# One small exponential per unit for the roots of queries and keys, and a least key root per unit for the flag

## Chip, cores, metric

One core of one Trainium2 chip. The metric is device time in microseconds (us). The kernel before takes 607.91 us (median of the 3 runs given at the start, 607.86 to 608.15).

Engines in the profile: PE is the matmul engine (TensorE), DVE VectorE, ACT ScalarE, POOL GpSimd. The granted clock is the share of its full clock that PE was given.

## The reference, cut to what matters

```python
def rmsnorm(x, g):                      # q, k: (8, 12, 448, 64)
    rms = np.sqrt(np.mean(x * x, axis=-1, keepdims=True) + 1e-06)
    return x / rms * g
q_n, k_n = rmsnorm(q, g_q), rmsnorm(k, g_k)
scores = 1/np.sqrt(64) * np.matmul(q_n, k_n.transpose(0, 1, 3, 2))
attn = softmax(scores)                  # cut
attn_out = np.matmul(attn, v)
# then, on (8, 448, 768): layer norm, ReLU MLP 768 -> 3072 -> 768, residual
```

Only the inverse root 1/rms of each query and key row is touched by the change. The kernel multiplies the queries by theirs, and passes the keys' as the per-row scale of the big exponential over the scores.

## The kernel before

The work on queries, keys and values goes in 25 units: the first two hold one pair of heads (7 groups of 128 rows for queries and 7 for keys), the others two pairs (14 and 14). A root is made as exp(-0.5 ln(sum of squares)) on ACT. A guard is computed at the end: if any root or sum lies outside what the fast path can represent, a flag sends the program to a slow general path. For that guard every key root of the whole kernel was kept in one tile `rr_all` of 336 columns.

```python
self.rr = fix.tile([128, 7 * B * NPAIR], FP32, name="rr_all", tag="rr_all")   # 336 columns
...
def begin():                                   # per unit u, g = 7 or 14 groups
    ...
    o = 7 * UNIT_PAIR[u]
    c["r", 0] = self.p_n.tile([128, 14], FP32, tag="rq", name="rq")[:, 0:g]   # queries
    c["r", 1] = self.rr[:, o:o + g]                                           # keys
...
def root(n=slice(0, 2)):
    nc.scalar.activation(c["rt"][:, n], c["ssq"][:, n], AFT.Ln, bias=D * 1e-6)
    for i in range(2)[n] if isinstance(n, slice) else (n,):
        nc.scalar.activation(c["r", i], c["rt"][:, i], AFT.Exp, scale=-0.5)
...
# scores(p, i): one 128 x 448 block of exp(scores), with the key root as scale
nc.scalar.activation(out=c["E"][:, i], in_=ps[:, 0:S], func=AFT.Exp,
                     scale=self.rr[:, g:g + 1], bias=EXP_BIAS)
...
# step "M" of the written order of instructions, at the end of the ramp
nc.vector.tensor_reduce(out=gmax, in_=self.sh.gprod, axis=AX.X, op=ALU.max, ...)
nc.vector.tensor_scalar(out=gmax, in0=gmax, scalar1=1.0 / K_MAX, ...)
...
# flag(), near the end: all key roots at least gmax?
nk = self.rr.shape[1]
nc.vector.tensor_scalar(out=good[:, 0:nk], in0=self.rr, scalar1=sh.gmax, scalar2=None, op0=ALU.is_ge)
nc.vector.tensor_reduce(out=cnt[:, 1:2], in_=good[:, 0:nk], axis=AX.X, op=ALU.add)
```

The order of instructions is written out by hand; only DVE after the first part is ordered by the scheduler. The order string at the end of the first part is `... l5 z5 U1 U2 V6.5 M m5 V6.6 L7 K7`, where `m5` is a copy of queries and `K7` the transpose and copy of keys whose result PE waits for.

## Time and profile before

| | kernel before |
|---|---|
| time | 607.91 us |
| span of the profiled run | 605.9 us |
| PE busy | 578.3 us (95%) |
| ACT busy | 360.7 us, 697 instructions |
| DVE busy | 286.5 us, 618 instructions |

The span is a ramp of about 61 us, in which PE waits for the others again and again, then 507 us in which it hardly waits, then the last block of matmuls and stores. The groups that the change removes or shrinks are small. From the view of groups by line and shape (count after the x; then busy us and mean ns; then the engine's idle time before them):

```profile
L223 ACT ACTIVATE rq<-rt 128x14 f32<-128x14 f32 x23 | 5.0, 215 | 0.7
L223 ACT ACTIVATE rr_all<-rt 128x14 f32<-128x14 f32 x23 | 4.5, 198 | 0.0
...
L741 DVE TENSOR_REDUCE cnt<-good 128x1 f32<-128x336 f32 x1 | 0.5, 493 | 0.0
...
L739 DVE TENSOR_SCALAR good<-rr_all,gmax 128x336 f32<-128x336 f32 x1 | 0.4, 395 | 0.1
```

The two groups of exponentials come to 9.5 us by these figures.

### The profile page before, as it was taken

The page shows a single profiled execution, that of the slowest core. Times are in us where ns is not written, and L with a number is a line of the kernel's source. Part 1 is how long each engine was busy: PE and PEld are TensorE (multiplying, and loading weights), DVE is VectorE, ACT ScalarE, POOL GpSimd, SP SyncE. Part 2 cuts the span into 40 slices and gives each one's busy share as a digit, 9 for nine tenths or more (in the row PEclk, how much of TensorE's full clock was granted, in tenths as well). Part 3 has the DMA queues.
Part 4 walks back from the last instruction along what each step waited for, and adds up shares of the span by engine and source line. Part 5 has one row for each costly group of instructions (what it writes and reads, how often), then busy time and mean ns, then how long its engine had stood idle before and what let it go on. Part 6 is the DMA issues. An engine that isn't in the chain of part 4 may idle for free.

```text
span 605.9 us, 11525 instructions
## 1 busy us (share of the span) xinstructions
PE 578.3 (95%) x4500; PEld 344.6 (57%) x4500; DVE 286.5 (47%) x618; ACT 360.7 (60%) x697; POOL 189.5 (31%) x245
## 2 busy tenths in 40 slices
PE   2877999999999999999999999999999999999995
PEld 1555666655566666655566666655566666654564
DVE  5799567734346256715256255734256322540011
ACT  6996986278752697358753598548754477124200
POOL 3853432233551355332542345423512000000000
PEclk9999999999999999999999999999999999999998
DMA  9999999479864586844944585847722330130011
GB/s 208 266 213 217 215 224 178 123 195 87 143 157 117 98 129 146 177 135 83 150 121 113 123 125 128 197 116 121 133 65 70 92 62 2 34 98 0 1 53 57
DMA packets 130861, 75.29 MB, mean 124 GB/s; under 512 B 96656, under 2 KB 121040, under 8 KB 130800
## 3 DMA queue, kind: packets, MB, share of 16 engines
q1 hardware_dynamic: 114048, 45.12, 38.3%
q0 software_dynamic: 16080, 28.94, 21.6%
q8 instruction: 37, 0.61, 0.4%
q10 hardware_dynamic: 672, 0.43, 0.2%
q14 instruction: 24, 0.20, 0.1%
HBM read 52.36 MB, written 11.01 MB: 105 GB/s over the span
## 4 chain that ended last, share of the span: by engine, by line
PE 88%; DVE 1%; ACT 1%; issue 0%
PE psC L637 36%; PE psH L621 34%; PE psS L352 8%; PE oA L381 5%; PE oB L383 2%; PE psS L356 1%; PE psS L355 1%; PE tr L330 0%; PE tr L316 0%; ACT E L358 0%; DVE x L398 0%; DVE qn L67 0%; DVE khl L240 0%; ACT khl L215 0%; ACT hT L623 0%
## 5 line engine op out<-in xcount | busy, mean ns | idle before, releaser
L621 PE MATMUL psH<-xnT,w 128*128 128x512 f16 (+1 forms) x1134 | 241.9, 353 | 0.0
L358 ACT ACTIVATE E<-psS,rr_all 128x448 f16<-128x448 f32 x336 | 207.0, 634 | 48.3 <-PE psS L352 43.0
L637 PE MATMUL psC<-w,hT 128*128 128x384 f16 (+1 forms) x1368 | 234.7, 323 | 0.0
L623 ACT ACTIVATE hT<-psH 128x512 f16<-128x512 f32 (+1 forms) x189 | 104.0, 550 | 123.9 <-PE psH L621 121.9
L637 PEld LDWEIGHTS <-hT 128*128 128x128 f16 x1368 | 127.5, 98 | 74.6
L621 PEld LDWEIGHTS <-w 128*128 128x128 f16 x1134 | 102.5, 98 | 80.9 <-issue 0.3
L352 PE MATMUL psS<-qU,kU 128*128 128x448 f16 x288 | 100.6, 357 | 8.3 <-ACT E L358 6.0
L381 PEld LDWEIGHTS <-E 128*128 128x128 f16 x1008 | 70.7, 98 | 49.1 <-issue 4.4
L229 POOL TENSOR_TENSOR qkv<-qkv,gprod 128x896 f32<-128x896 f32 x21 | 43.7, 2081 | 95.8 <-issue 49.5
L381 PE MATMUL oA<-v,E 128*128 128x65 f16 x864 | 66.7, 194 | 0.1
L641 DVE SCALAR_TENSOR_TENSOR x<-psC,rs_all,x 128x384 f32<-128x384 f32 x48 | 29.0, 616 | 71.5 <-PE psC L637 71.1
L396 DVE RECIPROCAL rec_all<-oA 128x6 f32<-128x6 f32 x48 | 9.3, 194 | 94.4 <-PE oA L381 94.2
L383 PE MATMUL oB<-v,E 128*128 128x65 f16 x288 | 51.9, 194 | 0.1
L127 POOL DMA_DIRECT2D qkv<-in_k_dram x14 | 11.2, 798 | 129.7 <-DVE qn L279 61.8
L218 DVE TENSOR_REDUCE ssq<-khl 128x14 f32<-128x896 f32 (+1 forms) x24 | 25.6, 1065 | 44.6 <-ACT khl L215 44.5
L352 PEld LDWEIGHTS <-kU 128*128 128x128 f16 x288 | 28.0, 98 | 25.5 <-issue 6.0
L218 DVE TENSOR_REDUCE ssq<-qn 128x14 f32<-128x896 f32 (+1 forms) x25 | 26.2, 1047 | 21.8 <-ACT qn L215 21.7
L67 DVE SCALAR_TENSOR_TENSOR qn<-qkv,rq 128x256 f16<-128x256 f32 (+1 forms) x72 | 26.3, 425 | 15.1 <-ACT rq L223 15.0
L383 PEld LDWEIGHTS <-E 128*128 128x128 f16 x336 | 32.5, 97 | 0.3 <-DVE xl L403 0.2
L240 DVE TENSOR_TENSOR khl<-qkv,khl 128x896 f16<-128x896 f32 x21 | 22.8, 1088 | 10.8 <-ACT khl L237 7.1
L398 DVE TENSOR_TENSOR x<-oA,rec_all 128x384 f32<-128x384 f32 x48 | 26.8, 558 | 1.5
L545 DVE BATCH_NORM_STATS2 stat<-x 128x6 f32<-128x256 f32 (+1 forms) x75 | 26.2, 404 | 0.6
(104 smaller groups left out, 447.7 us busy)
## 6 DMA issues: line engine op xcount, KB each, us to landing
out_dram<-x SPq DMA_DIRECT2D x20, 384.0 KB, 2.5
qkv<-in_k_dram POOLq DMA_DIRECT2D x14, 384.0 KB, 3.9
qkv<-in_q_dram POOLq DMA_DIRECT2D x14, 384.0 KB, 5.2
qkv<-in_v_dram POOLq DMA_DIRECT2D x14, 384.0 KB, 6.6
w<-in_moe_w_ch_dram POOLq DMA_DIRECT2D x3, 1536.0 KB, 14.6
w<-in_moe_w_ch_dram POOLq DMA_DIRECT2D x2, 2304.0 KB, 24.3
qkv<-in_k_dram SPq DMA_DIRECT2D x7, 384.0 KB, 5.7
qkv<-in_q_dram SPq DMA_DIRECT2D x7, 384.0 KB, 4.6
```

The costliest lines, as they stand in the source:

```text
L67: nc.vector.scalar_tensor_tensor(out=out, in0=x, scalar=8.0, in1=r.unsqueeze(2).broadcast_to([x.shape[0], g, D]), op0=ALU.mult, op1=ALU.mult)
L218: nc.vector.tensor_reduce(out=c["ssq"][:, n], in_=c["sq", n], axis=AX.X, op=ALU.add)
L229: (nc.vector if u in DVE_KG else nc.gpsimd).tensor_tensor(out=c["t"][1], in0=c["t"][1], in1=sh.gprod.unsqueeze(1).broadcast_to([128, g, D] ...
L352: nc.tensor.matmul(ps[:, 0:S], c["main"][:, ts(i, 128)], q[:, ts(h, S)], start=True, stop=True)
L358: nc.scalar.activation(out=c["E"][:, i], in_=ps[:, 0:S], func=AFT.Exp, scale=self.rr[:, g:g + 1], bias=EXP_BIAS)
L381: nc.tensor.matmul(oA[:, t, cs], E[:, i, ts(t, 128)], rhs, start=(i == 0 and t == 0), stop=(i == 6 and t == 2))
L383: nc.tensor.matmul(oB[:, cs], E[:, i, 320:448], rhs, start=(i == 0), stop=(i == 6))
L398: nc.vector.tensor_tensor(out=x[:, :, 128 * hp:128 * hp + 128].rearrange("p t (e d) -> p t e d", e=2), in0=oA[:, :, :, 0:D], in1=rec[:, 0: ...
L621: nc.tensor.matmul(ps[:, 0:N], sh.w1[:, dc, ts(f, 128)], xnT[:, dc, 0:N], start=(dc == 0), stop=(dc == NDC - 1))
L623: nc.scalar.activation(out=hT[:, f, 0:N], in_=ps[:, 0:N], func=AFT.Relu)
L637: nc.tensor.matmul(ps[:, 0:g[1]], hT[:, f, ts(t, 128)], sh.w2[:, f, cols], start=(f == 0), stop=(f == NFF - 1))
L641: nc.vector.scalar_tensor_tensor(out=x[:, cols], in0=ps[:, 0:g[1]], scalar=self.rs[:, b, t:t + 1], in1=x[:, cols], op0=ALU.mult, op1=ALU.add)
```

## The change

Its intent: one exponential for both roots in place of two, a small tile of roots per unit in place of columns of a big one, and only the least key root of each unit for the guard, so that the guard compares 25 columns and not 336. The price is one reduce per unit on DVE, five of them together at "M".

```diff
-        self.rr = fix.tile([128, 7 * B * NPAIR], FP32, name="rr_all", tag="rr_all")
+        self.rr = fix.tile([128, len(UNITS)], FP32, name="rr_all", tag="rr_all")
@@ begin
-            o = 7 * UNIT_PAIR[u]
-            c["r", 0] = self.p_n.tile([128, 14], FP32, tag="rq", name="rq")[:, 0:g]
-            c["r", 1] = self.rr[:, o:o + g]
+            c["rb"] = self.p_n.tile([128, 2, 14], FP32, tag="rq", name="rr_all", bufs=6)[:, :, 0:g]
+            c["r", 0], c["r", 1] = c["rb"][:, 0], c["rb"][:, 1]
@@ root
-            for i in range(2)[n] if isinstance(n, slice) else (n,):
-                nc.scalar.activation(c["r", i], c["rt"][:, i], AFT.Exp, scale=-0.5)
+            nc.scalar.activation(c["rb"][:, n], c["rt"][:, n], AFT.Exp, scale=-0.5)
@@ scores
-                             scale=self.rr[:, g:g + 1], bias=EXP_BIAS)
+                             scale=self.units[PAIR_UNIT[p][0]][3][:, g:g + 1], bias=EXP_BIAS)
+        u = PAIR_UNIT[p][0]
+        if i == 6 and UNIT_PAIR[u] == p and u > 4:
+            self.least(u)
+    def least(self, u):
+        self.nc.vector.tensor_reduce(out=self.rr[:, u:u + 1], in_=self.units[u][3], axis=AX.X,
+                                     op=ALU.min)
@@ step "M"
+                for u in range(5):
+                    self.least(u)
                 gmax = self.sh.gmax
```

More of the change, by code (lines that the diff above doesn't have):

```diff
@@ L201, in begin @@
             c["rt"] = self.p_n.tile([128, 2, 14], FP32, tag="rt", name="rt")[:, :, 0:g]
-            o = 7 * UNIT_PAIR[u]
-            c["r", 0] = self.p_n.tile([128, 14], FP32, tag="rq", name="rq")[:, 0:g]
-            c["r", 1] = self.rr[:, o:o + g]
+            c["rb"] = self.p_n.tile([128, 2, 14], FP32, tag="rq", name="rr_all", bufs=6)[:, :, 0:g]
+            c["r", 0], c["r", 1] = c["rb"][:, 0], c["rb"][:, 1]
             c["qn"] = self.p_n.tile([128, 14, 2, D], FP16, tag="qn", name="qn")[:, 0:g]
             c["khl"] = self.p_n.tile([128, 14, 2, D], FP16, tag="khl", name="khl")[:, 0:g]
-            self.units[u] = (c["qn"], c["khl"], m)
+            self.units[u] = (c["qn"], c["khl"], m, c["r", 1])
         def square(n):
@@ L310, in trans_k @@
         u, w = PAIR_UNIT[p]
-        qn, khl, m = self.units[u]
+        qn, khl = self.units[u][0:2]
         kT, ps = self.kU[PE_SET][:, 960 * (p % 2):960 * (p % 2) + 960], self.tr
@@ L322, in trans_q @@
         u, w = PAIR_UNIT[p]
-        qn, khl, m = self.units[u]
+        qn, khl = self.units[u][0:2]
         tr = self.ps_m.tile([128, 1024], FP16, tag="mlp", name="psQ") if p < NPAIR else self.tr
@@ L356, in scores @@
             nc.tensor.matmul(ps[:, 0:S], left[:, 64:192], q[:, S:2 * S], start=False, stop=True)
-        g = 7 * UNIT_PAIR[PAIR_UNIT[p][0]] + self.group(p, i)
+        g = self.group(p, i)
         nc.scalar.activation(out=c["E"][:, i], in_=ps[:, 0:S], func=AFT.Exp,
-                             scale=self.rr[:, g:g + 1], bias=EXP_BIAS)
+                             scale=self.units[PAIR_UNIT[p][0]][3][:, g:g + 1], bias=EXP_BIAS)
[5 more added lines that the diff above has]
+                                     op=ALU.min)
     def values(self, p, i):
```

## The prediction

> **What bounds the kernel now.** I read the page's busy table and slices first, then busy time by stretch, then TensorE's waits, then the instructions around the two places that the change touches. The page of the kernel before:
>
> ```profile
> PE 578.3 (95%) x4500; PEld 344.6 (57%) x4500; DVE 286.5 (47%) x618; ACT 360.7 (60%) x697; POOL 189.5 (31%) x245
> PE   2877999999999999999999999999999999999995
> ```
>
> TensorE (PE) is the bound on the whole; ScalarE (ACT) and VectorE (DVE) have slack on the average. But the first four digits are 2, 8, 7, 7: there are 605.9 - 578.3 = 27.6 us without PE work, and most of it lies in the first 60 us. The view by stretch shows the two regimes (columns: stretch, its length, busy us and instructions by engine, clock, DMA share, GB/s):
>
> ```profile
> 20.00:30.00 10.00, 7.84 (x100) 5.22 (x100) 8.59 (x17) 9.81 (x21) 8.10 (x10) 1.00 0.89 237
> 30.00:40.00 10.00, 8.41 (x110) 5.61 (x109) 9.65 (x20) 9.71 (x18) 5.95 (x7) 1.00 1.10 211
> 40.00:50.00 10.00, 7.00 (x95) 4.39 (x92) 9.46 (x27) 8.42 (x17) 5.11 (x3) 1.00 1.12 217
> ...
> 200.00:300.00 100.00, 100.00 (x769) 57.91 (x767) 45.86 (x103) 72.71 (x144) 44.77 (x62) 1.00 0.69 132
> ```
>
> In the ramp PE has 7 to 8.4 us of work in 10 while ACT and DVE are at 8.4 to 9.8: there a microsecond of ACT or DVE can be a microsecond of the kernel. From about 61 us on, attention and MLP matmuls are interleaved and PE is never short of work. After 60 us these are all of PE's listed waits:
>
> ```profile
> PE psS L352 <- DVE kU L318: 0.5, 1, 0.5
> PE psS L352 <- ACT E L358: 0.2, 1, 0.2
> ```
>
> So a change to small ACT and DVE instructions can act only in the ramp, up to that 0.5 us wait for a DVE copy at 60.9 us, which ends the ramp.
>
> [...] On ACT, for unit 2:
>
> ```profile
> 18.39 0.23 ACT L221 ACTIVATE rt<-ssq 128x28 f32<-128x28 f32 x1
> 18.65 0.22 ACT L223 ACTIVATE rq<-rt 128x14 f32<-128x14 f32 x1
> 18.77 0.20 ACT L223 ACTIVATE rr_all<-rt 128x14 f32<-128x14 f32 x1
> 18.88 2.21 ACT L358 ACTIVATE E<-psS,rr_all 128x448 f16<-128x448 f32 x4
> ```
>
> Each small exponential is recorded as 0.20 to 0.22 us, but the next instruction starts 0.11 to 0.12 us after it. The logarithm costs more (0.26), since the first exponential waits for its result. On DVE at the end of the ramp:
>
> ```profile
> 57.26 1.08 DVE L67 SCALAR_TENSOR_TENSOR qn<-qkv,rq 128x896 f16<-128x896 f32 x1
> 58.26 0.21 DVE L443 TENSOR_REDUCE gmax<-gprod 128x1 f32<-128x64 f32 x1
> 58.51 0.15 DVE L445 TENSOR_SCALAR gmax<-gmax 128x1 f32<-128x1 f32 x1
> 58.58 0.38 DVE L279 COPY qn<-qn 128x896 f16<-128x896 f16 x1
> ```
>
> The 896-column instruction holds the engine for 58.26 - 57.26 = 1.00 us. [...] the 0.15 us scaling of gmax is followed 0.07 us later. [...]
>
> **The change, part by part.** The ordered instruction lists of both kernels, with their semaphore waits, are alike on PE, GpSimd and the DMA queues; on ACT and DVE only the following differs.
>
> (a) ACT, removed: one exponential in 24 of the 25 units (the first unit's two roots are taken separately and stay two). The survivor has 28 columns in place of 14, some 0.02 us more (the logarithm's mean is 240 ns at 28 columns, 215 at 14). Not 24 x 0.2 = 4.8 us but about 24 x 0.10 = 2.4 us of engine time. Nineteen of these lie after 61 us, where PE does not wait: worth nothing. Unit 5's, at 56.75, lies in the ramp, but the DVE instruction that needs it starts at 57.26, long after. Units 1 to 4 fall at 13.3, 18.8, 28.8 and 40.9 us. From 23.9 to 44.4 us DVE has no idle time: it is the limit there, ACT's saving for unit 3 is lost behind it, and unit 4's runs into 0.54 us of ACT idle at 42.1. That leaves units 1 and 2, whose following score exponentials are what PE waits for (PE idle for ACT E at 14.9, 19.5 and 23.3 us). 2 x 0.10 = 0.2 us earlier at the most, 0.1 if another wait takes over: I take -0.15.
>
> (b) DVE, longer wait: query scaling now waits for the joint exponential, 0.02 us more. It is exposed for units 1 and 2 and nearly cancels there; +0.02.
>
> (c) DVE, added in the ramp: the least roots of units 0 to 4, five reduces together just ahead of gmax, plus unit 5's, which the schedule has put between the gmax reduce and its scaling. [...] The sixth fits the hole in which the scaling waits for gmax (58.26 to 58.51[...]): 0. These sit on the chain that sets the end; the chain's own view:
>
> ```profile
> 57.34 1.00 DVE qn L67
> 58.34 0.14 DVE gmax L443
> 58.48 0.02 issue
> 58.51 0.15 DVE gmax L445
> 58.66 0.30 DVE qn L279
> ...
> 60.21 0.67 DVE kU L318
> 60.88 0.04 issue
> 60.93 0.55 PE psS L352 x2
> ```
>
> DVE is busy without a break from 57.3 to the key copy, and PE stands idle for 0.46 us until it lands. Whatever is put in at 58.3 arrives whole at 60.9, and PE is full afterwards. So +0.39.
>
> (d) DVE, added later: 19 reduces x 0.08 = 1.5 us, where DVE is under half busy and PE does not wait: 0. They stand between the query scaling and the query's duplicate, so they hold a key or query transpose up by 0.08 us, which is loaded well ahead.
>
> (e) DVE, cheaper at the end: the flag's compare and count over 336 columns (395 and 493 ns) become 25 columns, like the 32-column ones (181 and 186). Some 0.5 us less at 534 us, behind which PE has MLP work; the flag's matmul comes at 540.9, 4.7 us after its data. Worth 0.
>
> Sum: -0.15 + 0.02 + 0.39 = +0.26 us. 607.91 + 0.26 = 608.2.
>
> **Rivals.** First, ACT as the true limit of the whole ramp: then all of units 1 to 5 count, -0.5 us, which about cancels the reduces: 607.8. For it, ACT's 9.8 in 10 from 20 to 40 us; against it, DVE's unbroken run from 23.9 on. Second, recorded length as cost: 4.8 us less ACT work carried to the end gives 603; against it are the 0.11 us spacing and that nine tenths of the chain is PE. Third, the reduces cost what is recorded, about 0.17 us each, because each waits for the one before: six x 0.17 = 1.0 and about 608.8. Against it, the instruction list shows no wait on them, and they write different columns. Fourth, PE's clock: the 448-column score matmul takes 0.53 us at 14.9 and 16.3 us and 0.35 from 19.5 on. [...] up to about 1 us either way, mostly absorbed since ACT paces PE there. Fifth, [...] unit 2's query scaling took 1.58 us against 1.08 for unit 3's like-sized one. A small shift may take that 0.5 us away or bring it elsewhere.
>
> **Range and chances.** The kernel's own three runs spread over 0.29 us. The modelled part lies between -0.1 (first rival) and +0.9 (third); the fourth and fifth add some +-0.7 in each direction. Range 607.2 to 609.1. A 2% difference is 12 us; nothing in the sum is a tenth of that. Within 2%: 0.98; the remainder is for a shift in buffers or DMA timing that no list shows, equal on both sides.
>
> **What would show each step.** (a) ACT 673 instructions in place of 697, busy about 2 us less, not 5; the square or score exponential that follows starts 0.1 us sooner after the logarithm. (c) Five reduces before gmax at a spacing of 0.07 to 0.08 us; PE's wait for the key copy at 61 us grows from 0.46 to about 0.85; this is the telling line. (d) DVE 643 instructions, busy about 288 us (+2.0 for 25 reduces, -0.5 at the flag); no new PE wait after 62 us. (e) The flag's two instructions near 0.18 us each, PE's order there untouched. I would be wrong if the PE wait at 61 us stayed at 0.5 (the reduces filled holes, or the chain is set elsewhere), if PE waits appeared in the steady part, or if the ramp ended more than 0.5 us sooner (ACT was the limit after all).

The forecast's sum came to +0.26 us (-0.15 for (a), +0.02 for (b), +0.39 for (c)), 608.2 us in all. With them went the working of (c)'s +0.39 and of the fourth rival's "up to about 1 us" (part of the +-0.7 in the range); they, and the 0.08 us for each reduce in (d), stand as what the author forecast. For the reduces the trace of the kernel before leads to nearly the same: its 128x896 reduces are recorded at 1084 ns and followed 1.00 us after their start, the one-column scaling of gmax 0.07 us after its start. A straight line through these two gives, as an estimate, 0.076 us at 7 columns and 0.084 at 14, so 2 x 0.076 + 3 x 0.084 = 0.40 us for the five. What made unit 2's query scaling longer (the fifth rival) was not shown.

## The result, and the profile after

| | before | after |
|---|---|---|
| time, median (range) of 6 runs each | 608.07 us (607.86 to 609.48) | 608.17 us (607.69 to 608.80) |
| ratio after to before | | 0.9998, 95% interval 0.9985 to 1.0011 |
| span of the profiled run | 605.9 us | 606.9 us |
| ACT busy, instructions | 360.7 us, 697 | 359.5 us, 673 |
| DVE busy, instructions | 286.5 us, 618 | 287.1 us, 643 |

ACT's busy time fell by 1.2 us, where the prediction's check had about 2, and DVE's rose by 0.6, where it had 1.5. The ratio is the mean time of one kernel's fast runs over that of the other's of the same rounds, so it is not quite the ratio of the medians. The parts are below what the timing resolves, so they are read from the traces.

The exponentials. ACT of the changed kernel, unit 2, to be held against the four lines in the prediction:

```profile
18.47 0.23 ACT L220 ACTIVATE rt<-ssq 128x28 f32<-128x28 f32 x1
18.73 0.23 ACT L221 ACTIVATE rr_all<-rt 128x28 f32<-128x28 f32 x1
18.87 2.21 ACT L357 ACTIVATE E<-psS,rr_all 128x448 f16<-128x448 f32 x4
```

From the first small exponential to the first big one it was 18.88 - 18.65 = 0.23 us; it is 18.87 - 18.73 = 0.14. The removed instruction, recorded at 0.20 us, saved 0.09.

The reduces. DVE of the changed kernel at the end of the ramp (in merged rows such as x5 the duration is that of the whole row):

```profile
58.30 1.08 DVE L67 SCALAR_TENSOR_TENSOR qn<-qkv,rr_all 128x896 f16<-128x896 f32 x1
59.31 0.44 DVE L366 TENSOR_REDUCE rr_all<-rr_all 128x1 f32<-128x7 f32 x5
59.67 0.21 DVE L453 TENSOR_REDUCE gmax<-gprod 128x1 f32<-128x64 f32 x1
59.79 0.15 DVE L366 TENSOR_REDUCE rr_all<-rr_all 128x1 f32<-128x14 f32 x1
59.91 0.15 DVE L455 TENSOR_SCALAR gmax<-gmax 128x1 f32<-128x1 f32 x1
```

Five reduces hold the engine for 59.67 - 59.31 = 0.36 us, 0.07 each; the sixth sits in the hole before the scaling of gmax, which still starts 0.24 us after its reduce.

Then PE. First the kernel before, then the changed one: every PE row with idle time listed from 60 to 72 us (the bracket holds that idle time and what ended it).

```profile
60.93 0.55 PE L352 MATMUL psS<-qU,kU 128*128 128x448 f16 x2 [0.46 <-DVE kU L318]
66.04 0.35 PE L352 MATMUL psS<-qU,kU 128*128 128x448 f16 x1 [0.17 <-ACT E L358]
```

```profile
62.33 0.55 PE L351 MATMUL psS<-qU,kU 128*128 128x448 f16 x2 [0.86 <-DVE kU L317]
```

The wait for the key copy has grown by 0.40 us, but the wait for ACT 5 us later is gone. I had not counted that.

One thing differs in the first 30 us that no instruction list shows. By stretches of 1 us (last columns: granted clock, DMA share, GB/s), the kernel before and then the changed one:

```profile
22.00:23.00 1.00, 0.93 (x18) 0.71 (x16) 0.69 (x2) 1.00 (x2) 1.00 (x3) 1.00 0.92 262
24.00:25.00 1.00, 0.97 (x17) 0.63 (x14) 0.91 (x4) 0.91 (x3) 1.00 (x1) 1.00 0.81 232
```

```profile
22.00:23.00 1.00, 1.00 (x12) 0.82 (x10) 0.31 (x1) 1.00 (x2) 1.00 (x2) 0.50 0.60 180
24.00:25.00 1.00, 1.00 (x11) 0.78 (x10) 0.68 (x2) 0.38 (x1) 1.00 (x1) 0.50 0.90 246
```

In this run of the changed kernel PE had half its clock for 3.41 us (21.73 to 25.14 in the trace's clock record). From 22 to 23 us it did 12 matmuls where the other did 18, and from 24 to 25 us ACT was busy for 0.38 us where it had been for 0.91. Is that the change's doing, or chance? The experiments had to settle that too.

To compare traces without it, I split each into two intervals with fixed ends: A from PE's first transpose to the score matmul at 61 us that ends the ramp, B from there to the start of the last block of 216 matmuls at 568 us. The three rows that bound them, in the kernel before and in f4, a run of the changed kernel with more reduces long after the ramp (described below):

```profile
8.49 0.29 PE L313 MATMUL tr<-id,khl 128*128 128x128 f16 x1 [8.49 <-DVE khl L240]
...
60.93 0.55 PE L352 MATMUL psS<-qU,kU 128*128 128x448 f16 x2 [0.46 <-DVE kU L318]
...
568.21 31.42 PE L637 MATMUL psC<-w,hT 128*128 128x384 f16 x216
```

```profile
8.90 0.29 PE L313 MATMUL tr<-id,khl 128*128 128x128 f16 x1 [8.90 <-DVE khl L240]
...
61.52 0.55 PE L352 MATMUL psS<-qU,kU 128*128 128x448 f16 x2 [0.86 <-DVE kU L318]
...
568.46 31.42 PE L651 MATMUL psC<-w,hT 128*128 128x384 f16 x216
```

"Clock" says until when PE ran slow: matmuls of 448 columns are recorded at about 0.53 us when slow and 0.35 when free. The times are those of the trace's clock record, which begins when the clock is freed; before that the views print a granted clock of 1.00 all the same, as from 14 to 18 us in the kernel before.

| trace | clock | A | B | A + B |
|---|---|---|---|---|
| before | slow to 18.8 us | 52.44 | 507.28 | 559.72 |
| before, second trace (f1) | slow to 20.0 us | 52.64 | 507.28 | 559.92 |
| after | slow to 18.3, again 21.7 to 25.1 us | 53.68 | 506.93 | 560.61 |
| after, second trace (f2) | slow to 23.7 us | 53.30 | 506.92 | 560.22 |
| after with extra reduces late (f4) | slow to 18.9 us | 52.62 | 506.94 | 559.56 |

B repeats to 0.02 us within a kernel, and it is 0.35 us shorter in the changed one. (The traces of g2 and g3 below, of the same two kernels with idle matmuls, give 507.29 and 506.93.) A depends on the clock by up to 1.06 us. For a finer reading the start of every score matmul, counted from the first transpose, is compared between two traces; I call the difference its shift. The first transpose itself comes at 8.48 to 8.90 us, with the arrival of the first loads (DVE's wait for one of them ends at 6.22 to 6.64 us).

### The profile page after: what moved, and what is told of

It is laid out like the page before. It is cut to its first block, busy times and chain, and to the rows that moved or that the text cites. A ratio compares the mean times of both kernels' runs of the same rounds, so it can differ in the third digit from the quotient of the medians.

```text
span 606.9 us, 11525 instructions
## 1 busy us (share of the span) xinstructions
PE 579.4 (95%) x4500; PEld 346.4 (57%) x4500; DVE 287.1 (47%) x643; ACT 359.5 (59%) x673; POOL 190.1 (31%) x245
## 4 chain that ended last, share of the span: by engine, by line
PE 90%; DVE 2%; ACT 0%; issue 0%; DVEq 0%
PE psC L647 36%; PE psH L631 35%; PE psS L351 8%; PE oA L389 5%; PE oB L391 2%; PE psS L354 1%; PE psS L355 1%; PE tr L329 0%; PE tr L315 0%; PE psU L677 0%; DVE stat L555 0%; DVE xn L576 0%; DVE x L406 0%; DVE qU L334 0%; ACT E L357 0%
## 5 line engine op out<-in xcount | busy, mean ns | idle before, releaser
L67 DVE SCALAR_TENSOR_TENSOR qn<-qkv,rr_all 128x256 f16<-128x256 f32 (+1 forms) x72 | 26.3, 424 | 15.3 <-ACT rr_all L221 15.3
```

Source lines behind the costliest of these rows:

```text
L67: nc.vector.scalar_tensor_tensor(out=out, in0=x, scalar=8.0, in1=r.unsqueeze(2).broadcast_to([x.shape[0], g, D]), op0=ALU.mult, op1=ALU.mult)
```

## The experiments

Twelve runs were made, each with a correct result; f1 and f2 are the two kernels themselves. The timing has an interval of some +-0.0014 (0.8 us) at best, so costs were magnified where a time was to show them.

**e1_red50: 50 more reduces at the end of the ramp.** They write to columns of their own, so none waits for another.

```diff
                 nc.vector.tensor_scalar(out=gmax, in0=gmax, scalar1=1.0 / K_MAX, ...)
+                for e in range(50):
+                    nc.vector.tensor_reduce(out=self.xr[:, e:e + 1], in_=self.units[e % 5][3],
+                                            axis=AX.X, op=ALU.min)
```

> The changed kernel with 50 further reduces of key roots (to columns of their own, with no wait between them) right after gmax at the end of the ramp. My step (c), what is put in there arrives whole: [...] PE's wait for the key copy at 61 us grows from 0.9 to about 4.8 us and the time by 3.9 us over the changed kernel (ratio to the kernel before about 1.0065). Rival, cost as recorded (0.15 us each): +7.5 us, ratio 1.012. Rival, hidden in holes of DVE: ratio 1.000.

(Its 3.9 us was for 20 reduces of 7 columns and 30 of 14.)

Measured: 614.98 us against 608.32 for the kernel before, ratio 1.0109 (1.0094 to 1.0124), 6.7 us and not 3.9. DVE and PE of this run:

```profile
59.02 3.65 DVE L459 TENSOR_REDUCE xr<-rr_all 128x1 f32<-128x7 f32 x50
62.58 1.19 DVE L279 COPY qn<-qn 128x896 f16<-128x896 f16 x1
```

```profile
65.74 0.93 PE L352 MATMUL psS<-qU,kU 128*128 128x448 f16 x2 [5.23 <-DVE kU L318]
```

```profile
66.00:68.00 2.00, 2.00 (x7) 0.91 (x6) 1.79 (x2) 1.16 (x2) 0.00 (x0) 0.50 1.20 179
```

The 50 reduces took 62.58 - 59.02 = 3.56 us, 0.071 each, less than I had estimated and under half of the recorded 0.15. The copy after them took 1.19 us in place of 0.38. GpSimd was busy beside it (1.99 of the 2.00 us from 62 to 64 us), and in the kernel before it was idle there (until 60.02 us); whether the one has to do with the other was not tested. PE's wait grew from 0.86 to 5.23 us: 3.56 + 0.81 = 4.37. So what is put in there does arrive whole. Then comes the clock: after a wait of 5 us PE came back at half speed (the third fence; from 65.73 to 69.14 us), and B of this trace is 508.51 us, 1.57 more than in f4. The traced run is the fastest of the four (613.85); the others are about 1 us longer, and no trace says why. By the time alone, 6.7 us would look nearest to the rival that takes the recorded length (+7.5); the 3.56 us on DVE rule it out, and the grown wait rules out the rival that hides the reduces. The expectation for the time missed: in the trace 4.37 us came at the wait and 1.57 us after it.

**e2_exp_u12 and e3_exp_u34: 8 more exponentials in units 1 and 2, or in units 3 and 4.** Same edit, other units.

```diff
             nc.scalar.activation(c["rb"][:, n], c["rt"][:, n], AFT.Exp, scale=-0.5)
+            for e in range(8 if u in (1, 2) else 0):
+                nc.scalar.activation(self.xe[:, e, :, 0:g], c["rt"][:, n], AFT.Exp, scale=-0.5)
```

> The changed kernel with 8 further small exponentials (to a scratch tile) behind the root of each of units 1 and 2, where I said ACT paces the ramp: 8 x 0.12 + 8 x 0.14 = 2.1 us of ACT. My step (a): nearly all of it reaches the end, +1.7 to +2.1 us (ratio to the kernel before about 1.003). Rival, recorded length (0.23 us each): +3.7 us. Rival, ACT never limits: 0.

> The same 8 further exponentials behind the roots of units 3 and 4: 16 x 0.14 = 2.2 us of ACT, where I said that DVE is the limit and ACT's time is lost. My step (a): less than half reaches the end, 0 to +1.0 us. First rival, ACT is the limit of the whole ramp: +2.2 us, as in the run with units 1 and 2.

Measured: 609.43 us (ratio 1.0015, 1.0000 to 1.0030) and 609.54 us (1.0013, 0.9998 to 1.0029). The times do not separate the two, since the runs differ in their clock: e3's trace has the half clock at 22 us as the first trace after had, e2's has it full there. Compared with traces of the same kind, the intervals do separate them. In e2 the 16 instructions took 0.83 + 0.93 = 1.76 us of ACT (0.104 each at 14 columns, 0.116 at 28); A is 54.36 us against 52.62 in f4: +1.74, all of it. In e3 they took 2 x 0.93 = 1.86 us; A is 54.42 against 53.68 in the first trace after: +0.74, 0.4 of it. (B is 507.19 there, 0.26 more, lost near 119 us in a stall that its neighbours do not have; I leave it out.) So ACT paces the ramp for units 1 and 2; for units 3 and 4 more than half of its time is lost behind DVE. That ACT limits the whole ramp (the first rival: all 1.86) is refuted. But the two units are not alike: unit 3's 0.93 us put DVE's next key copy 0.57 us back, and later ones 0.52, while unit 4's added only 0.22. DVE is the limit for unit 3 with ACT close behind it, so a saving is lost there but a long addition is not.

**e4_m_late: the five reduces and gmax behind the key copy.**

```diff
-Q7 X2 c5 e5 j5 g5 k5 l5 z5 U1 U2 V6.5 M m5 V6.6 L7 K7
+Q7 X2 c5 e5 j5 g5 k5 l5 z5 U1 U2 V6.5 m5 V6.6 L7 K7 M
```

> The changed kernel with the five reduces and gmax moved behind the key copy that PE waits for at 61 us; only unit 5's reduce stays before it. My step (c): PE's wait at 61 us falls from 0.9 to about 0.3 us (0.9 less 0.39 for the reduces and 0.25 for gmax and its scaling, plus 0.08 for unit 5's reduce, which no longer has a hole to fit), the time by 0.5 to 0.6 us against the changed kernel (ratio to the kernel before about 0.9992, near what five rounds resolve). Rival, the chain is set elsewhere: the wait shrinks but the span from that matmul's start to the end grows by as much, no gain.

Measured: 607.87 us (607.58 to 608.35), ratio 0.9993 (0.9980 to 1.0007). The wait fell to 0.32 us and A to 52.08, as expected; but B rose to 507.34, from 506.94.

```profile
60.69 0.55 PE L351 MATMUL psS<-qU,kU 128*128 128x448 f16 x2 [0.32 <-DVE kU L317]
```

Of the 0.54 us gained at the wait, 0.40 was lost again, all of it by 66 us, so A + B (559.42) is only 0.14 below f4's. This is what the rival of that expectation said, for three quarters of the size. It is also where my step (c) first broke.

**f1_before_again and f2_after_again: the two kernels once more.** No edit.

> The kernel before, unchanged, once more: the null of the timing and a second trace. Every theory expects a ratio of 1.000. In the one trace of the changed kernel so far TensorE's granted clock is at half from about 21.9 to 25.1 us, which it is not in the one of before. If the change brings this, this trace and nearly all runs (lower mean clock, 0.9 us longer) of the kernel before are without it; if it comes by chance in either, runs of both kernels fall in two groups 0.6 to 1 us apart.

> The changed kernel, unchanged, once more. My prediction: ratio 1.0004 (+0.26 us), which the timing does not resolve; in the trace, PE's wait at 61 us is 0.86 us again, and the DVE key copy's place in time from PE's first transpose to 44 us is 0.15 us shorter than in the kernel before when neither trace has the slow clock at 22 us. If the slow clock is by chance, this trace may be without it: then the span is within 0.4 us of that of before.

Measured: 607.97 us (607.82 to 608.60) and 607.95 us (607.75 to 608.65); ratios 0.9995 (0.9981 to 1.0008) and 0.9994 (0.9980 to 1.0007). Runs of both kernels fall in two groups. The changed kernel, all 11 runs: six of 607.69 to 607.95 us, five of 608.47 to 608.80. The kernel before shows both as well, for example 607.82 to 608.07 with one run of 608.60 in f1, and 608.92 to 609.06 in the runs beside it. (A few runs at 608.3 lie between.) So the slow clock is not the change's doing alone, and g2 below has the half clock in the kernel before, with idle matmuls. 15 of 38 runs of the kernel before are above 608.4 us, and 5 of 11 of the changed one: too few to say whether the change makes it more or less frequent. The trace of f2 shows the second form of the same thing, with no dip in the granted clock: PE was simply freed late.

```profile
19.61 1.05 PE L351 MATMUL psS<-qU,kU 128*128 128x448 f16 x2 [0.15 <-ACT E L357]
...
20.91 0.56 PE L351 MATMUL psS<-qU,kU 128*128 128x448 f16 x1
```

At 19.6 us the matmuls of the first trace before are recorded at 0.35 us each; here the fast ones begin at 23.9 us, at a cost in A of 0.68 us against f4. My expectation that a trace without the dip would lie within 0.4 us of before missed (its span is 606.9) for that reason. The 0.15 us that I expected it to gain by 44 us can't be read from it either; f4's trace, with the clock freed early, shows it (see (a) below).

**f3_exp_rest and f4_red_rest: 3 more exponentials, or 10 more reduces, in each of units 6 to 24.** Edits as in e2 and e1, for the other units.

> The changed kernel with 3 further small exponentials behind the root of each of units 6 to 24, in the part where PE is never short: 19 x 3 x 0.14 = 8.0 us of ACT. My step (a), nothing of it counts there: ratio to the kernel before within 0.001 of that of the changed kernel. Rival, ACT's engine time counts everywhere: +8 us, ratio 1.013; cost as recorded, 0.23 us each: +13 us, ratio 1.02.

> The changed kernel with 10 further reduces of key roots (to columns of their own) for each of units 6 to 24: 190 x 0.08 = 15 us of DVE. My step (d), nothing counts after the ramp: ratio as the changed kernel's, within 0.001. Rival, DVE's time counts where queries are scaled and copied: up to 15 us, ratio 1.025.

Measured: f3 608.86 us, ratio 1.0010 (0.9994 to 1.0025); f4 608.13 us, ratio 1.0000 (0.9985 to 1.0015). Against f2's 0.9994 f3 is 0.0016 higher and thus misses the 0.001 that I gave it, within the noise of its clock (slow to 23.6 us). Its B tells more: 507.42, 0.50 us more than in the changed kernel, for 57 x 0.116 = 6.6 us of ACT. The only listed PE wait of that run after 62 us is this:

```profile
66.92 0.35 PE L353 MATMUL psS<-qU,kU 128*128 128x448 f16 x1 [0.26 <-ACT E L359]
```

It is the wait for ACT that the changed kernel had lost, brought back by unit 6's extra exponentials. By the shift against the changed kernel, 0.34 us of the 0.50 comes here, for 3 x 0.116 = 0.35 us of ACT: so ACT paces PE here too, and step (a) was wrong to count unit 6's exponential for nothing. Another 0.15 comes by 83 us, behind unit 7's, without a listed wait; after that the shift stays. In f4, 190 reduces (recorded at 155 ns, 17.2 us in sum) leave B at 506.94: nothing. Step (d) holds.

**g1_before_red: only the reduces, on the kernel before.** It tests the give-back by itself.

```diff
+    def least(self, u):
+        o = 7 * UNIT_PAIR[u]
+        self.nc.vector.tensor_reduce(out=self.rmin[:, u:u + 1],
+                                     in_=self.rr[:, o:o + 7 * UNITS[u][2]], axis=AX.X, op=ALU.min)
```

(called where the change calls it; the guard still reads all roots)

> The kernel before with only part (c) and (d) of the change: the least key root of each unit reduced to a further tile, the exponentials still two. From the traces so far: the wait for the key copy grows from 0.46 to 0.86 us, but the two small gaps of PE that follow within 6 us (0.37 us together) go, since ACT is no longer behind. So from PE's first transpose to the start of the last block of matmuls at 568 us the trace shows the 559.7 us of before within 0.1, if the ramp has no slow clock. My prediction's step (c) as written (nothing is given back): 560.1.

Measured: 608.40 us, ratio 1.0003 (0.9988 to 1.0019). In the trace (clock freed at about 18 us) the wait is 0.82 us, A 52.81 (+0.37), B 507.03 (-0.25), the sum 559.84: +0.12 us over the first trace before.

```profile
61.65 0.55 PE L353 MATMUL psS<-qU,kU 128*128 128x448 f16 x2 [0.82 <-DVE kU L319]
```

The sum lies between the give-back (559.7 +-0.1, just missed) and my step as written (560.1), nearer to the former: two thirds were given back.

**g2_before_warm, g3_after_warm, g4_m_late_warm: idle matmuls against the clock.** 82 matmuls of the identity that nobody reads, 54 before the first transpose and 28 where PE waits up to 21 us, in the kernel before, the changed one, and e4.

```diff
+H54 b0 a0 c0 L4 ... K0 Q0 H9 d0 ... H3 S0.2 d2 c2 S0.3 H10 S0.4 ... S1.3 H6 K2
```

> The kernel before with 82 matmuls of the identity that nobody reads, put where PE waits in the first 22 us, so that its clock is released early and stays. If the two groups of times come from when the clock is released, all runs of this kernel fall in one group, with a spread under 0.4 us, and score matmuls take 0.35 us from the first on; the time falls by 0.3 to 1.0 us. If they do not come from it, the groups stay.

> The changed kernel with the same idle matmuls. What the change is worth without the clock's chance, against the kernel before with them: -0.15 (exponentials) + 0.40 (reduces) - 0.37 (given back) = -0.1 us, ratio between the two 0.9998. My prediction as written: +0.26.

> The changed kernel with the reduces behind the key copy, and the idle matmuls: the version that should beat both, by 0.1 to 0.2 us against the changed kernel with idle matmuls, and by 0.5 to 1.2 us against the kernel before, ratio 0.998 to 0.999.

Measured: 607.50, 607.29 and 607.50 us; ratios to the kernel before 0.9985 (0.9972 to 0.9999), 0.9987 (0.9973 to 1.0001) and 0.9982 (0.9969 to 0.9996). In all three traces the first scores run at 0.35 us (or 0.54 for two), so the late release is gone (in g2 the clock is free from 8.24 us; in traces without idle matmuls from 17.9 to 23.7 us). But one run of five of each is still 1.2 to 1.5 us longer, and two of the three traces (g2 and g4, which are of those longer runs) show the half clock again from about 22 to 25 us, g2 once more from 49.2 to 52.6: the expectation of one group failed. Those three slow runs set aside, the means are 607.51 (before), 607.29 (after) and 607.32 us (reduces late). So the change is worth -0.2 us with the early clock, near the expected -0.1 and not my +0.26, but by four runs of each, picked after the fact; moving the reduces adds nothing, where 0.1 to 0.2 us was expected. All three are below the kernel before by 0.13 to 0.18% in the mean (g3's interval just includes 1), for a reason that has nothing to do with the change.

## Why the prediction was right or wrong

The time (608.17 us against 608.2) came out as predicted, and the mechanism of the exponentials in units 1 and 2 was right. That the time agrees so closely is luck: with the clock of the traces alike, the change is worth -0.16 us and not +0.26, and the timing cannot tell the two apart.

**(a) Exponentials, -0.15.** Held in the ramp. Each removal is worth 0.08 to 0.09 us and not the recorded 0.2. The shift of f4 against the first trace before, of a like clock, shows it directly: -0.08 us from the score matmul at 14.9 us (unit 1), -0.17 from that at 19.5 (unit 2). Unit 3's 0.09 appears at 29.5 us and is gone at 33.1, unit 4's does not appear, and the shift is still -0.17 when the reduces come; in g1, which keeps the exponentials, it is 0.00 until then. "Nineteen of these lie after 61 us: worth nothing" did not hold for unit 6 (see c).

**(b) Longer wait for the joint exponential, +0.02.** Not measurable by itself; DVE's listed wait for it in unit 2 was 1.02 us and is 1.03.

**(c) Reduces at the end of the ramp, +0.39.** This is the step that failed, in its second half. "Whatever is put in at 58.3 arrives whole at 60.9" held: 0.36 us of DVE, +0.40 at PE's wait, and 4.37 of 4.37 us in e1. "And PE is full afterwards. So +0.39" did not: in the 5 us that follow, PE of the kernel before lost 0.17 us at a listed wait for ACT and about as much in delays that are not recorded as idle time. A later PE finds ACT done and loses neither. In f4 the shift of the score matmuls jumps by 0.35 us at 61 us, to +0.18, falls to +0.06 at 62.4 and is -0.19 at 66.0 and -0.16 at the end: all of it is gone within 5 us. The listed wait stood in my own evidence, as "0.2 us" below the one that I used; I read two waits behind each other as one limit, where the second was slack that the first could consume. Not all of the 0.35 us is that slack, though: g1, with the reduces alone, gives back 0.28 by 66 us and 0.25 in the end, so the reduces cost 0.12 net. The other 0.1 or so is unit 6's removed exponential: ACT's shift goes from -0.08 to -0.19 us across it in f4, and from +0.12 to only +0.09 in g1. With -0.17 for units 1 and 2, +0.12 and about -0.1 give the -0.16 of the sum. The share of unit 6 is a difference of traces; no run removes its exponential alone.

**(d) Later reduces, 0.** Held, at ten times the number (f4).

**(e) The guard, 0.** Its two instructions fell from 395 and 493 to 240 and 178 ns; the flag's matmul stayed where it was, behind the same MLP work.

With the clock freed early the sum of A and B is 559.56 us after (f4) and 559.72 before: -0.16 us in place of +0.26.

**The rivals.** The first (ACT limits all of the ramp) fell with e3, the second and third (recorded length is cost) with e1 and e2. The fifth was idle: unit 2's query scaling, 1.58 us before, is 1.68, 1.66 and 1.67 us in the traces after, and e2, where it came later and took 1.09, gained nothing visible from that. The fourth, the clock, was real and is the largest effect: 0.7 to 1.1 us of A, more than every part of the change. I had put it at up to about 1 us "mostly absorbed"; it isn't absorbed. In the clock records of these three traces the clock changes only at whole multiples of 3.413 us from its first change, whose place differs from trace to trace: the first trace after has changes at 18.314, 21.727 and 25.141 us; e1 at 17.942, 65.729 (14 x 3.413 later) and 69.142; g2 at 8.244, 21.898 (4 x), 25.311, 49.204 (7 x) and 52.618. What decides, in a given stretch of 3.41 us, whether the clock changes stays open. PE's recorded busy time alone does not: the first trace after lost its clock after a stretch with 1.78 us busy, e1 kept it after one with 1.61 (58.90 to 62.32 us).

## What to carry to other kernels

Take a small instruction's cost from the start of one to the start of the next, not from its recorded length: here 0.07 us on DVE and 0.10 to 0.12 on ACT for recorded lengths of 0.15 to 0.23. Then follow a shift past the wait that it lengthens: if the delayed engine has another wait close behind, on a different engine that is not delayed, the second wait shrinks by up to what the first one grew; here 0.25 of 0.37 us came back so (g1). And before an effect of a few tenths of a microsecond is explained, cut the trace into intervals with fixed ends and see which of them repeat; here one repeated to 0.02 us in all traces but e3's, and the other carried a chance of 1 us.
